# Retention, then a cosine-gated feed-forward: a state tile per head parity, a conversion ahead of two masks, another one part later

## The chip, the cores and the metric

One core of a Trainium2 chip. Times are device microseconds of whole executions. A profiled execution has a span as well (first to last instruction), some 2 us shorter. The chain (the work that ended last, followed back from its end) and the timelines start a group of matmuls at slightly different times, so starts are compared within one view; they are from the chain unless the text says otherwise. Ratios are the mean time of one kernel's fast runs over that of the kernel before in the same rounds, so not quite the ratio of the medians quoted beside them.

Engines: PE is TensorE's matmuls, PEld its weight loads, DVE is VectorE, ACT ScalarE, POOL GpSimd. In a profile line, [0.48 <-DVE stb L491] says that the engine stood idle for 0.48 us until VectorE's instruction of line L491 on tile stb ended; the waits are inferred from semaphore events.

## The reference

```python
def _attn_ref(q, k, v):                       # (4, 8, 768, 64) each
    gamma = 1.0 - 2.0 ** (-5.0 - np.arange(H))
    for t in range(S):
        state = gamma[None, :, None, None] * state + np.einsum('bhd,bhe->bhde', k[:, :, t], v[:, :, t])
        y[:, :, t] = scale * np.einsum('bhd,bhde->bhe', q[:, :, t], state)
def _moe_ref(x, w_in, w_out):                 # (3072, 512), (512, 2048), (2048, 512)
    h = x @ w_in
    return (h * np.cos(h)) @ w_out
```

The retention is computed in chunks of 128 steps: masked scores within a chunk, and a state (64 x 64 per head) from chunk to chunk. Its output is the feed-forward's x.

## The kernel before

A "pair" is one chunk of two batch entries; twelve pairs in a row. Two heads share the 128 partitions: head parity j uses partitions 64j to 64j + 63. The state sums up in one PSUM tile, `st_ps`, as large as each of the seven general banks (512 fp32 per partition), so that here a PSUM tile and a bank are the same thing. Copies bring it to SBUF as bf16 weights for the next pair; the other parity's partitions stay zero.

```python
banks = Banks([psum.tile([128, 512], FP32, name=f"bank{i}") for i in range(7)], clk)
st_ps = psum.tile([128, 2, HP, D], FP32, name="st_ps")
stb = [sb([128, 2, HP, 128], BF16, f"stb{i}") for i in range(2)]
...
def state_out(p, copy_st):                    # later pairs: both copies on one engine
    for j in range(2):
        copy_st(out=stb[(p + 1) % 2][ts(j, 64), :, :, ts(j, 64)], in_=st_ps[ts(j, 64)])
...
it = stage_a(1, 0)                            # scores of pair 1
stage_m(1, it, (0,))                          # mask on VectorE
stage_s(0, None)                              # state after pair 0
for j, cp in enumerate((nc.scalar.copy, nc.vector.tensor_copy)):
    cp(out=stb[1][ts(j, 64), :, :, ts(j, 64)], in_=st_ps[ts(j, 64)])     # L491
stage_m(1, it, (1,))
stage_m(1, stage_a(1, 1))
half_y(0, 0); half_y(0, 1); half_y(1, 0)      # (three lines in the kernel, with clock lines between)
first_f((0, 1), 0)                            # first feed-forward matmuls, L366
...
pair_f(2, 0); conv_k(4, True)                 # two cosines, then k of pair 4 on ScalarE
pair_f(2, 1); conv_k(5, True)                 # two cosines, then k of pair 5
attend(3)                                     # scores and four masks of pair 3
```

`pair_f` makes two PSUM banks of w_in products (L353), each with a cosine on ScalarE (L331) and a product on VectorE (L335) that frees the bank. The cut joins some lines and leaves out the lines that feed the time model (`clk`). The tile framework places all waits. The line numbers in the profiles are the kernel's own.

## Time and profile before

| | kernel before |
|---|---|
| median of 6 runs in the rounds of the result | 208.16 us (207.82 to 208.64) |
| span of the profiled run | 205.8 us |
| TensorE busy, and its share of the chain | 97%, 92% |
| VectorE, ScalarE busy | 55%, 56% |
| first state copies (L491) | ScalarE 12.58 to 13.17 us, VectorE 13.19 to 13.88 us |
| first feed-forward matmuls (L366) | 15.21 us |

From 15.21 us to its last matmul, at 202.7 us, TensorE waits for no other engine on the chain. Only an earlier start, or a new gap, can move that point; the last copy out (202.73) and its store follow. Two weight loads in the timeline of weight loads (columns: start, duration, engine, line, operation) say how finely the framework tracks the state tile:

```profile
13.34 0.11 PEld L283 LDWEIGHTS <-stb 128*64 128x64 bf16 x1
13.94 0.11 PEld L283 LDWEIGHTS <-stb 128*64 128x64 bf16 x1 [0.48 <-DVE stb L491]
```

The first load takes parity 0's columns while VectorE is still writing parity 1's into the same tile; only the second load waits for VectorE.

### The profile page before, as it was taken

How to read it: one execution, taken by the hardware profiler on the slowest of the kernel's cores; microseconds unless marked ns; L12 is line 12 of the kernel's file. 1: busy time of each engine (PE TensorE's matmuls, PEld its weight loads, DVE VectorE, ACT ScalarE, POOL GpSimd, SP SyncE). 2: the span in 40 equal slices, each digit the busy share in tenths (PEclk: the TensorE clock that was granted, in tenths of full speed). 3: DMA queues.
4: the chain of work that ended last, by engine and by line, in shares of the span. 5: the costliest groups of instructions: out<-in, count | busy, mean ns of one | idle time of the engine just before them, and what ended most of it. 6: DMA issues, size and time to landing. Idle time of an engine off the chain costs nothing.

```text
span 205.8 us, 4101 instructions
## 1 busy us (share of the span) xinstructions
PE 199.2 (97%) x1631; PEld 113.0 (55%) x1631; DVE 113.3 (55%) x188; ACT 114.3 (56%) x191; POOL 92.4 (45%) x99
## 2 busy tenths in 40 slices
PE   7889999999999999999999999999999999999993
PEld 2458554558897555556454466444465444444453
DVE  4885884532968545769784366844467233344000
ACT  7675882259887536787446466453554654553120
POOL 8999338399999479979930730000000000000000
PEclk9999999999999999999999999999999999999999
DMA  6999999979999997999999905101101101110212
GB/s 155 352 243 198 217 244 286 341 139 294 319 187 255 338 127 132 312 298 229 251 371 362 194 29 127 53 6 49 51 3 53 51 15 39 51 51 5 99 51 102
DMA packets 33571, 34.34 MB, mean 167 GB/s; under 512 B 23376, under 2 KB 25680, under 8 KB 33552
## 3 DMA queue, kind: packets, MB, share of 16 engines
q0 software_dynamic: 7824, 22.29, 39.2%
q1 hardware_dynamic: 24544, 11.44, 23.6%
q10 hardware_dynamic: 1184, 0.36, 0.7%
q8 instruction: 12, 0.20, 0.4%
q14 instruction: 7, 0.06, 0.1%
HBM read 27.26 MB, written 6.29 MB: 163 GB/s over the span
## 4 chain that ended last, share of the span: by engine, by line
PE 92%; POOL 3%; DMA 2%; DVE 1%; issue 0%; ACT 0%; POOLq 0%
PE bank L388 39%; PE bank L342 32%; PE bank L353 7%; PE bank L261 3%; PE bank L283 3%; PE bank L288 3%; DMA vf<-in_v_dram 2%; PE bank L366 2%; PE bank L408 2%; PE st_ps L305 1%; POOL qf L130 1%; POOL kf L137 1%; POOL vs L204 1%; PE bank L232 0%; POOL kf L130 0%; POOL vf L130 0%
## 5 line engine op out<-in xcount | busy, mean ns | idle before, releaser
L335 DVE TENSOR_TENSOR gt<-bank,cosb 128x512 bf16<-128x512 f32 x96 | 65.1, 689 | 59.4 <-ACT cosb L331 59.2
L331 ACT ACTIVATE cosb<-bank,halfpi 128x512 bf16<-128x512 f32 x96 | 65.0, 687 | 50.0 <-PE bank L342 44.5
L388 PE MATMUL bank<-w_out_sb,gt 128*128 128x512 bf16 x368 | 89.8, 379 | 0.0
L342 PE MATMUL bank<-xt,w_in 128*128 128x512 bf16 x304 | 75.3, 380 | 0.0
L388 PEld LDWEIGHTS <-gt 128*128 128x128 bf16 x368 | 35.4, 98 | 41.1
L342 PEld LDWEIGHTS <-w_in 128*128 128x128 bf16 x304 | 33.9, 114 | 30.5
L270 DVE TENSOR_TENSOR am<-bank,mask 128x512 bf16<-128x512 f32 x48 | 30.5, 682 | 4.0 <-PE bank L261 4.0
L204 POOL TENSOR_TENSOR vs<-vf,gk 128x512 bf16<-128x512 f32 x21 | 21.4, 1046 | 11.3 <-DMA vf<-in_v_dram 9.5
L197 POOL TENSOR_TENSOR qk<-qf,gq 128x512 bf16<-128x512 f32 x18 | 18.8, 1064 | 8.1 <-DMA out_dram<-ob 3.3
L395 ACT COPY ob<-bank 128x512 f32<-128x512 f32 x23 | 13.4, 587 | 14.8 <-PE bank L388 14.4
L210 ACT CAST qk<-kf 128x512 bf16<-128x512 f32 x24 | 13.9, 616 | 11.1 <-DMA kf<-in_k_dram 11.1
L292 ACT CAST xt<-bank 128x512 bf16<-128x512 f32 x24 | 13.0, 591 | 8.3 <-PE bank L288 8.3
L353 PE MATMUL bank<-xt,w_in 128*128 128x256 bf16 x128 | 14.6, 273 | 0.0
L353 PEld LDWEIGHTS <-w_in 128*128 128x128 bf16 x128 | 13.9, 113 | 0.8 <-issue 0.2
L288 PE MATMUL bank<-am,vs 128*64 128x128 bf16 x192 | 11.7, 220 | 0.4 <-DVE am L270 0.4
L317 DVE CAST stb<-st_ps 64x512 bf16<-64x512 f32 x14 | 9.6, 685 | 3.9 <-PE st_ps L305 3.7
L283 PEld LDWEIGHTS <-stb 128*64 128x64 bf16 x160 | 8.8, 109 | 4.7 <-issue 3.8
L283 PE MATMUL bank<-qkt,stb 128*64 128x128 bf16 x160 | 10.8, 222 | 0.3 <-DVE stb L491 0.3
L137 POOL DMA_DIRECT2D kf<-in_k_dram x9 | 10.5, 1172 | 0.0
L288 PEld LDWEIGHTS <-vs 128*64 128x64 bf16 x192 | 9.9, 110 | 0.5 <-issue 0.4
L130 POOL DMA_DIRECT2D vf<-in_v_dram x8 | 7.1, 885 | 4.9 <-DMA w_out_sb<-in_moe_w_out_dram 4.9
L137 POOL DMA_DIRECT2D qf<-in_q_dram x8 | 9.2, 1151 | 0.0
(49 smaller groups left out, 98.7 us busy)
## 6 DMA issues: line engine op xcount, KB each, us to landing
out_dram<-ob SPq DMA_DIRECT2D x23, 256.0 KB, 2.4
kf<-in_k_dram POOLq DMA_DIRECT2D x9, 512.0 KB, 6.3
qf<-in_q_dram POOLq DMA_DIRECT2D x8, 512.0 KB, 7.0
vf<-in_v_dram POOLq DMA_DIRECT2D x8, 512.0 KB, 8.1
vf<-in_v_dram POOLq DMA_DIRECT2D x8, 256.0 KB, 5.4
w_out_sb<-in_moe_w_out_dram POOLq DMA_DIRECT2D x4, 512.0 KB, 12.3
qf<-in_q_dram POOLq DMA_DIRECT2D x6, 256.0 KB, 7.2
w_in<-in_moe_w_in_dram POOLq DMA_DIRECT2D x3, 512.0 KB, 6.3
```

Of the source, the lines that this page charges most:

```text
L137: nc.gpsimd.dma_start(out=both[n][SLOT[p]].rearrange("p b h d -> p (b h) d"), in_=SRC[n][1][2 * bp : 2 * bp + 2, :, ds(c * C, C)].rearrang ...
L197: eng.tensor_tensor(out=qk[p % NB][:, b, 0], in0=qf[SLOT[p]][b], in1=bc(gq, p % NC), op=ALU.mult)
L204: eng.tensor_tensor(out=vs[p % NB][:, b], in0=vf[SLOT[p]][b], in1=bc(gk, p % NC), op=ALU.mult)
L210: nc.scalar.copy(out=qk[p % NB][:, b, 1], in_=kf[SLOT[p]][b])
L270: nc.vector.tensor_tensor(out=am[p % 2][b][j], in0=ap[j], in1=mask.unsqueeze(1).to_broadcast([128, HP, 128]), op=ALU.mult)
L283: nc.tensor.matmul(yp[ts(j, 64), a, :], lhsT=stb[p % 2][:, b, a, ts(j, 64)], rhs=qt(n, b, a), start=True, stop=False, skip_group_check=True)
L288: nc.tensor.matmul(yp[ts(j, 64), a, :], lhsT=vs[n][:, b, 2 * a + j, :], rhs=am[p % 2][b][j][:, a, :], start=(c == 0), stop=True, skip_grou ...
L331: nc.scalar.activation(out=cb, in_=bank, func=AF.Sin, bias=halfpi)
L335: nc.vector.tensor_tensor(out=out, in0=bank, in1=cb, op=ALU.mult)
L342: nc.tensor.matmul(bank, lhsT=w_in_t(i, f), rhs=xt[g % 2][:, i, :], start=(i == 0), stop=(i == KIN - 1))
L353: nc.tensor.matmul(bank[:, ts(e, 256)], lhsT=w_in_t(i, f + e), rhs=xt[g % 2][:, i, ts(hf, 256)], start=(i == 0 and e == 0), stop=(i == KIN ...
L388: nc.tensor.matmul(bank, lhsT=gt[g % 2][:, f, ts(j, 128)], rhs=w_out_sb[:, f, :], start=(f == 0), stop=(f == KOUT - 1))
```

## The change

Its intent: ScalarE and VectorE copy the first state side by side (part 1); the second v conversion of pair 2 fills VectorE's wait for scores (part 2); k of pair 5, whose transfer ScalarE stands waiting for, goes behind the next two cosines (part 3).

```diff
-    stb = [sb([128, 2, HP, 128], BF16, f"stb{i}") for i in range(2)]
+    stb = [[sb([128, 2, HP, 64], BF16, f"stb{i}_{j}") for j in range(2)] for i in range(2)]
...
-                        yp[ts(j, 64), a, :], lhsT=stb[p % 2][:, b, a, ts(j, 64)],
+                        yp[ts(j, 64), a, :], lhsT=stb[p % 2][j][:, b, a, :],
...
-        cp(out=stb[1][ts(j, 64), :, :, ts(j, 64)], in_=st_ps[ts(j, 64)])
+        cp(out=stb[1][j][ts(j, 64)], in_=st_ps[ts(j, 64)])
...
-            conv_v(2, nc.vector, (0,))
+            conv_v(2, nc.vector)
         elif u == 9:
             stage_m(2, stage_a(2, 0))
-            conv_v(2, nc.vector, (1,))
...
     pair_f(2, 1)
-    conv_k(5, True)
     attend(3)
     cq(4)
     stage_t_dma(4)
+    pair_f(2, 2)
+    conv_k(5, True)
...
-    pair_f(2, 2)
     pair_f(2, 3)
```

(The cuts leave out the memsets and the copies of later pairs, which change alike.)

More of the change, by code (lines that the diff above doesn't have):

```diff
@@ L178 @@
         nc.vector.memset(lgv[:, h : h + 1], lg[h])
-    for t in stb:
+    for t in stb[0] + stb[1]:
         nc.vector.memset(t, 0.0)
@@ L316, in state_out @@
         for j in range(2):
-            copy_st(out=stb[(p + 1) % 2][ts(j, 64), :, :, ts(j, 64)], in_=st_ps[ts(j, 64)])
+            copy_st(out=stb[(p + 1) % 2][j][ts(j, 64)], in_=st_ps[ts(j, 64)])
             clk.run("act" if copy_st == nc.scalar.copy else "dve", 0.65, clk.pe + 0.1)
```

## The prediction

> **What bounds the kernel now.** I read the page's busy shares first, then the chain that ended last (totals, then its opening in order of time), then VectorE, ScalarE and weight loads in that opening. The page's first lines:
>
> ```profile
> span 205.8 us, 4101 instructions
> PE 199.2 (97%) x1631; PEld 113.0 (55%) x1631; DVE 113.3 (55%) x188; ACT 114.3 (56%) x191; POOL 92.4 (45%) x99
> ...
> PE 92%; POOL 3%; DMA 2%; DVE 1%; issue 0%; ACT 0%; POOLq 0%
> ```
>
> TensorE is busy 97% of the span and carries 92% of the chain; VectorE holds 1% of it and ScalarE under half a per cent. So shortening work of VectorE, ScalarE or GpSimd pays only where such work is on the chain, and 1% is about 2 us. Where? The chain cut to its opening (columns: start in us, duration in us, engine, tile and line):
>
> ```profile
> 6.21 4.86 DMA vf<-in_v_dram
> 11.06 0.07 issue
> 11.13 1.05 POOL vs L204
> 12.19 0.04 issue
> 12.23 0.33 PE st_ps L305 x8
> 12.55 0.02 issue
> 12.58 0.59 ACT stb L491
> 13.17 0.02 issue
> 13.19 0.69 DVE stb L491
> 13.88 0.03 issue
> 13.91 0.70 DVE am L270
> 14.62 0.04 issue
> 14.66 0.22 PE bank L288
> ...
> 15.21 1.00 PE bank L366 x8
> ```
>
> The reader is to see two state copies (L491) **one after the other**: ScalarE 12.58 to 13.17, VectorE from 13.19. They read different partition halves of one PSUM tile, st_ps, and write different parts of one SBUF tile. Only after VectorE's copy comes the mask (13.91) for which TensorE waits (14.66). From 15.21 on the chain is TensorE alone: it never again leaves it for another engine, up to the end. In its dense stretches (chain, 30.13: 6.91 us for 32 matmuls of 512 columns) a matmul takes 6.91 / 32 = 0.216 us. Nothing in the change removes a matmul, so the only prize is an earlier start of the dense part.
>
> The other places that the change touches lie at 36.9 to 57.1 us, and there TensorE is busy 10.20 of 10.20 us and 10.00 of 10.00 us in the busy times by stretch. The waits that the change aims at are others':
>
> ```profile
> 38.72 0.68 DVE L204 TENSOR_TENSOR vs<-vf,gk 128x512 bf16<-128x512 f32 x1
> 40.02 1.29 DVE L270 TENSOR_TENSOR am<-bank,mask 128x512 bf16<-128x512 f32 x2 [0.61 <-PE bank L261]
> 41.22 0.68 DVE L204 TENSOR_TENSOR vs<-vf,gk 128x512 bf16<-128x512 f32 x1
> 42.18 1.29 DVE L270 TENSOR_TENSOR am<-bank,mask 128x512 bf16<-128x512 f32 x2 [0.28 <-PE bank L261]
> 52.55 1.14 ACT L210 CAST qk<-kf 128x512 bf16<-128x512 f32 x2 [0.70 <-DMA kf<-in_k_dram]
> ```
>
> VectorE waits 0.61 us for scores before it masks, and ScalarE stands 0.70 us in front of a k that has not landed, with its cosines queued behind. Neither delays TensorE today.
>
> **What the Trainium skill says.** (1) "PSUM — Partial Sum Buffer", section "PSUM bank collisions raise a hardware error": two engines on one bank and one group of 32 partitions collide, two reads included; different groups of one bank may be used together; the page calls guarding by whole bank "the simple version". The copies use partitions 0 to 63 and 64 to 127, so the chip would allow them together, but software that guards by bank puts one behind the other, whatever they write. The trace agrees with some such order: a 0.02 us step from one copy to the next. (2) "SBUF — State Buffer", section "Summary: rules for kernel authors": when VectorE has two SBUF inputs and GpSimd reads SBUF, the later one is blocked. The trace fits: GpSimd's q conversion took 1.44 us at 41.37 beside VectorE's v conversion (41.22 to 41.90), against 1.04 us at 39.85, which ran beside masks. (3) "TensorE: Matmul & The Clock Gate", section "Wait — 56ns, not 53.3ns?": 215.7 ns start to start for 512 columns when warm; the trace has 0.216 us, so the dense part has no slack inside.
>
> **Part 1, a state tile per head.** It leaves 18 further copies alike (14 on VectorE at 690 ns median, 4 on ScalarE at 582): from L317, both halves of a pair go to one engine, so no two engines meet. It makes four memsets of half the size from two: 128x512 words took 485 ns, 128x256 words 0.27 us, so 4 x 0.27 - 2 x 0.485 = 0.11 us more on VectorE before 2.4 us, where it then idles 1.67 us for q; ScalarE's tables behind it end at 4.54 and its next work comes at 4.77. Cost: nothing. The prize is L491 alone. If VectorE's copy starts with ScalarE's, at 12.58 or so rather than 13.19, the mask ends 0.61 us earlier. Before it, VectorE's last mask ends at 11.86 + 0.68 = 12.54, so VectorE is free. TensorE is at 13.40 with this product's first half, so 14.66 - 0.61 = 14.05 can be met. The next matmuls (15.21 becomes 14.60) need ScalarE's xt copies, which end at 13.38 + 1.07 = 14.45: 0.15 us of room. w_in's blocks land at 14.4, 15.8 and 18.4 (issue time plus time to landing) and would be needed at 14.6, 16.4 and 19.2. So the whole 0.61 us would reach the dense part.
>
> But does the split remove the wait? A tile-wide order on the destination is the intent's theory. The trace speaks against it: the first state weights (columns of head 0) were loaded at 13.34, **while** VectorE was still writing the same tile (13.19 to 13.88); only the second half's load waited, to 13.94. And vs of pair 0 was written by ScalarE (10.59) and GpSimd (10.45 to 11.06) at once. So dependencies within an SBUF tile look finer than the tile already, and disjoint parts don't wait. What the two copies still share, and the change leaves shared, is the source bank. I choose 6 chances in 10 that the order stays.
>
> **Part 2, v conversion ahead of the masks.** Same four VectorE instructions. The second conversion moves from 41.22 into the idle 0.61 us before the first mask: 38.72 + 2 x 0.68 = 40.08 instead of 40.02 for that mask, 0.06 us later; its product is needed at about 44, so TensorE sees nothing. v's second half has landed by 38.2 (29.06 + 9.1). GpSimd's second q conversion loses its collision: 1.44 - 1.04 = 0.40 us earlier, hence the k fetches behind it by up to that. Direct worth: 0.
>
> **Part 3, k of pair 5 one F part later.** The same two conversions (0.62 us each) go behind the first two cosines of the next part. The cosines no longer sit behind a 0.70 us DMA wait; but VectorE multiplies them only after its masks (to 54.98), and TensorE runs 51.12 to 54.83 for 32 matmuls without a stop. The transposes of pair 5 also need q, converted until 54.12 + 2.05 = 56.17, later than k's new end: the part starts at 51.12, its first two results are there at 52.0 and 52.9 (8 matmuls in 0.87 us each), the second cosine ends at 52.9 + 0.69 = 53.6, and two conversions at 53.6 + 1.14 = 54.7. So k is not late. Direct worth: 0 to 0.1 us.
>
> **Sum.** If the order at L491 goes: 0.61 us less at 14.6, carried on. Parts 2 and 3 then matter as passers-on: TensorE would be at pair 3's products at 54.2 instead of 54.8, and masks and xt copies must follow. k4 lands at 42.75 + 6.8 = 49.55 and gates ScalarE there, so without the 0.40 us from part 2 some of the gain would be lost again; I allow 0 to 0.2 us of loss. That gives 208.18 - 0.6 = 207.6. If the order stays: 208.18 - 0 to 0.1, say 208.15. Weighted: 0.4 x 207.6 + 0.6 x 208.15 = 207.93, rounded to **208.0** as the loss on the way speaks for the upper side.
>
> **The rivals.**
> - *The copies do go side by side* (4 in 10): for it, the step of 0.02 us after ScalarE shows no other cause, and a conservative comparison of two interleaved writes can't be excluded; against it, the weight load at 13.34. Time 207.6.
> - *The wait goes and another takes its place*: xt copies with 0.15 us of room at 14.45, or pair 3's masks and k4's landing at 49.55. Time 207.7 to 208.1.
> - *An engine becomes the bound*: VectorE and ScalarE are at 55 and 56% and lose nothing; k5 late could delay pair 5, whose scores come at 70.35. With 15 us between its conversion and those, unlikely. It would make 208.3 to 208.8.
> - *The two readers of one bank slow each other*: no sign to judge by; at most the 0.69 us grows and eats part of 0.61.
>
> **Range and chances.** The three runs before spread 207.82 to 208.45, so 0.3 us either way is noise, on both branches: 207.6 - 0.3 = 207.3 and 208.15 + 0.35 = 208.5. Two per cent is 4.2 us, seven times the largest prize, so "within 2%" is nearly sure: faster 0.01, same 0.98, slower 0.01.
>
> **What would show it.** In the changed trace: L491 on VectorE starts about 13.2 with a wait on ScalarE (order stays) or about 12.6 (gone). The first matmuls of line L366 start at 15.2 or at 14.6. VectorE shows two v conversions in a row near 38.7 and no wait of 0.7 us for k before the cosines near 52. If L366 starts at 14.6 and the span still is 205.8, the gain was given back between 37 and 57 us, and a TensorE gap must be there. The prediction is wrong if the order is gone and all else holds (nearer 207.5), or if bank choices, which a built-in time model makes anew for part 3, bring a TensorE stall that today is absent.

## The result, and the profile after

Median 208.02 us (207.54 to 208.44, 6 runs) against 208.16 us; ratio 0.9988, 95% interval 0.9968 to 1.0009. No difference can be told. The head of the changed kernel's page, and its chain by engine:

```profile
span 205.9 us, 4080 instructions
PE 197.2 (96%) x1609; PEld 112.5 (55%) x1631; DVE 113.4 (55%) x190; ACT 114.2 (55%) x191; POOL 92.0 (45%) x99
...
PE 91%; DMA 3%; ACT 2%; POOL 2%; issue 1%; DVE 1%; POOLq 0%; ACTq 0%
```

TensorE shows 1609 matmuls for 1631 weight loads: 22 records are missing, and the pieces of "issue" in this chain between matmuls are their places, not waits (0.16 us at 45.28 and then 1.67 us for 7 matmuls of L388, where the kernel before has 1.83 us for 8). VectorE has 2 instructions more, the memsets. The opening of the chain in order of time:

```profile
12.62 0.59 ACT stb L491
13.20 0.02 issue
13.23 0.69 DVE stb L491
...
13.95 0.70 DVE am L270
...
15.25 1.00 PE bank L366 x8
```

The two copies still stand one behind the other, now into two tiles, and VectorE's timeline names what it waited for:

```profile
13.23 0.69 DVE L491 CAST stb<-st_ps 64x512 bf16<-64x512 f32 x1 [0.62 <-ACT stb L491]
```

L366 starts 0.04 us later than before. The lines that parts 2 and 3 were aimed at, from the timelines of VectorE, GpSimd and ScalarE:

```profile
38.76 1.28 DVE L204 TENSOR_TENSOR vs<-vf,gk 128x512 bf16<-128x512 f32 x2
40.06 1.29 DVE L270 TENSOR_TENSOR am<-bank,mask 128x512 bf16<-128x512 f32 x2
...
41.44 1.04 POOL L197 TENSOR_TENSOR qk<-qf,gq 128x512 bf16<-128x512 f32 x1 [0.48 <-DVE am L270]
...
53.85 1.13 ACT L210 CAST qk<-kf 128x512 bf16<-128x512 f32 x2
```

Both v conversions run in a row, the masks follow at once, GpSimd's conversion is back from 1.44 to 1.04 us, and the k conversion no longer waits. All of it happened, and TensorE took none of it up. The k fetch of pair 4 behind GpSimd's conversion went out at 42.42 instead of 42.75 us, but took 7.2 instead of 6.8 us to land: at 49.6 us, no earlier than before.

### The profile page after: what moved, and what is told of

Same layout as the page of the kernel before. It is cut to its first block, busy times and chain, and to the rows that moved or that the text cites. A ratio compares the mean times of both kernels' runs of the same rounds, so it can differ in the third digit from the quotient of the medians.

```text
span 205.9 us, 4080 instructions
## 1 busy us (share of the span) xinstructions
PE 197.2 (96%) x1609; PEld 112.5 (55%) x1631; DVE 113.4 (55%) x190; ACT 114.2 (55%) x191; POOL 92.0 (45%) x99
## 4 chain that ended last, share of the span: by engine, by line
PE 91%; DMA 3%; ACT 2%; POOL 2%; issue 1%; DVE 1%; POOLq 0%; ACTq 0%
PE bank L388 39%; PE bank L342 32%; PE bank L353 7%; PE bank L261 3%; PE bank L283 3%; DMA kf<-in_k_dram 3%; PE bank L288 3%; PE bank L366 2%; PE bank L408 2%; PE st_ps L305 1%; POOL qf L130 1%; ACT vs L222 1%; ACT qkt L235 0%; PE bank L232 0%; POOL kf L130 0%
## 5 line engine op out<-in xcount | busy, mean ns | idle before, releaser
L388 PE MATMUL bank<-w_out_sb,gt 128*128 128x512 bf16 x357 | 88.2, 379 | 0.9 <-issue 0.5
L342 PE MATMUL bank<-xt,w_in 128*128 128x512 bf16 x294 | 74.1, 380 | 0.7 <-issue 0.3
L388 PEld LDWEIGHTS <-gt 128*128 128x128 bf16 x368 | 35.4, 98 | 41.0
L342 PEld LDWEIGHTS <-w_in 128*128 128x128 bf16 x304 | 33.7, 114 | 30.7
L204 POOL TENSOR_TENSOR vs<-vf,gk 128x512 bf16<-128x512 f32 x21 | 21.4, 1045 | 10.4 <-PE bank L342 4.9
L353 PE MATMUL bank<-xt,w_in 128*128 128x256 bf16 x128 | 14.6, 273 | 0.0
L353 PEld LDWEIGHTS <-w_in 128*128 128x128 bf16 x128 | 13.9, 113 | 0.9 <-issue 0.4
```

The lines of the kernel that those rows point to most:

```text
L204: eng.tensor_tensor(out=vs[p % NB][:, b], in0=vf[SLOT[p]][b], in1=bc(gk, p % NC), op=ALU.mult)
L342: nc.tensor.matmul(bank, lhsT=w_in_t(i, f), rhs=xt[g % 2][:, i, :], start=(i == 0), stop=(i == KIN - 1))
L353: nc.tensor.matmul(bank[:, ts(e, 256)], lhsT=w_in_t(i, f + e), rhs=xt[g % 2][:, i, ts(hf, 256)], start=(i == 0 and e == 0), stop=(i == KIN ...
L388: nc.tensor.matmul(bank, lhsT=gt[g % 2][:, f, ts(j, 128)], rhs=w_out_sb[:, f, :], start=(f == 0), stop=(f == KOUT - 1))
```

## The experiments

**Theory:** the shared PSUM bank of the *source* orders the copies. **Rival:** something else does, such as the shared destination or a fixed order of the two engines.

### Two PSUM tiles for the state, with and without the split destination (e1, e2), and the control (e3)

```diff
-    banks = Banks([... for i in range(7)], clk)
-    st_ps = psum.tile([128, 2, HP, D], FP32, name="st_ps")
+    banks = Banks([... for i in range(6)], clk)
+    st_ps = [psum.tile([128, 2, HP, D], FP32, name=f"st_ps{j}") for j in range(2)]
```

and `st_ps[j]` wherever parity j is written or read. So that the kernel keeps to eight PSUM banks in all, the general banks go from seven to six. e1 is this on the changed kernel, e2 on the kernel before with its one interleaved `stb` tile, e3 the changed kernel with six banks only.

> The changed kernel with one PSUM tile (bank) of state per head parity, and six instead of seven general banks. Theory (the shared PSUM bank orders the two copies): VectorE's first state copy starts within 0.1 us of ScalarE's (about 12.6 us instead of 13.2), the first L366 matmul at about 14.6 instead of 15.25 us; total 0.3 to 0.6 us less, or given back by the missing seventh bank. Rival (something else holds VectorE, such as the destination or a fixed order of the engines): VectorE still starts 0.6 us after ScalarE, L366 at 15.2.

> The kernel before, with its single interleaved destination tile kept, and the same two PSUM tiles. Theory: the copies are side by side here too, so a state tile per head is not needed for it: VectorE's copy starts at about 12.6 us, L366 at 14.6. Rival (the shared destination tile orders them as well): VectorE's copy stays 0.6 us behind ScalarE's here, though not in e1.

> The changed kernel with six general PSUM banks and nothing else: what the missing bank costs e1 and e2. Theory: the dense part is bound by TensorE with banks to spare; the first copies and L366 stay at 13.2 and 15.2 us, the total within 0.5 us of the changed kernel. Rival: the bank is needed and TensorE gets gaps, 1 us or more lost.

The two copies in the timelines of VectorE and ScalarE, e1 first, then e2:

```profile
12.50 0.69 DVE L491 CAST stb<-st_ps 64x512 bf16<-64x512 f32 x1
12.47 0.58 ACT L491 CAST stb<-st_ps 64x512 bf16<-64x512 f32 x1
```

```profile
12.45 0.69 DVE L491 CAST stb<-st_ps 64x512 bf16<-64x512 f32 x1
12.42 0.58 ACT L491 CAST stb<-st_ps 64x512 bf16<-64x512 f32 x1
```

Side by side, 0.03 us apart, with either destination. In e3, with six banks and one PSUM tile of state, VectorE again started 0.61 us after ScalarE and waited for it:

```profile
13.18 0.69 DVE L491 CAST stb<-st_ps 64x512 bf16<-64x512 f32 x1 [0.64 <-ACT stb L491]
```

So two source tiles, each in a bank of its own, are enough to lift the order, and a state tile per head parity is not needed for it. Whether the framework goes by the tile or by the bank, these runs don't separate, as each of them is a tile of one bank. L366 started at 14.48 and 14.43 us in e1 and e2, 15.13 in e3 and 15.18 in the changed kernel (timelines of TensorE). Both copies kept their durations beside each other. In e1 and e2 TensorE then waited 0.4 us for GpSimd's v conversion of pair 1 (L204) instead of the mask.

The totals did not follow. e1: ratio 1.0001 (0.9954 to 1.0048), e2: 0.9988 (0.9938 to 1.0039). e3 shows one reason, a line of its waits of TensorE (total us, times, longest):

```profile
PE bank L353 <- DVE gt L335: 0.9, 1, 0.9
```

With six banks TensorE waits for one near 51 us. e3's expectation, banks to spare and a total within 0.5 us, fell in the trace, and the rival came true there: its last matmul group started at 200.38 us instead of the changed kernel's 199.33, 1.05 us later. Timed, e3 was 1.0021 (0.9978 to 1.0065). e1 and e2 carry the same 0.9 us. e2 shows a second reason, in its chain:

```profile
11.98 8.30 DMA w_in<-in_moe_w_in_dram
```

The w_in block for L342, issued at 11.98 us, landed only 8.3 us later, and TensorE waited 1.3 us for it. In the kernel before the same fetch took 6.3 us. At 20.3 us it undid the earlier start. In e1's profile a third part came after TensorE's end: its last store took 2.7 us to land, 1.6 in the kernel before, so that 4.2 us passed from the last copy out (203.43) to the end of the span, against 3.1 (205.8 - 202.73). Its TensorE work ended 0.6 us later than the changed kernel's (last copies 203.43 and 202.86).

### Both first copies on one engine (e6)

```diff
-    for j, cp in enumerate((nc.scalar.copy, nc.vector.tensor_copy)):
+    for j, cp in enumerate((nc.vector.tensor_copy, nc.vector.tensor_copy)):
```

> The changed kernel with both first state copies on VectorE. Theory (the order makes ScalarE's help worthless: 0.58 + 0.69 us one after the other either way): VectorE copies from 12.6 to about 13.95 us, the same end as 13.92 in the changed kernel within 0.1 us, L366 within 0.1 us of 15.25. Rival (two engines do gain something): the end moves to 14.2 us or later.

VectorE copied from 12.33 to 13.74 us and L366 started at 15.07 in the chain: 0.18 us ahead of the changed kernel, where within 0.1 was expected. In the changed kernel ScalarE's copy first waits for its own qkt copy, which ends at 12.60; VectorE was free at the same time there (its masks end at 12.60), but in e6 already at 12.31, since its masks began at 11.03 instead of 11.32 us. So the start of this profile was 0.29 us ahead and the copies gave 0.11 of it back: 1.41 us on one engine (12.33 to 13.74), 1.30 us on two (12.62 to 13.92). While the order stands the second engine brings that 0.1 us at most, in one look.

### The mask into the forced wait (e4, e10 on the changed kernel; e5, e11 on the kernel before)

```diff
     stage_s(0, None)
+    stage_m(1, it, (1,))
     for j, cp in enumerate((nc.scalar.copy, nc.vector.tensor_copy)):
...
-    stage_m(1, it, (1,))
     stage_m(1, stage_a(1, 1))
```

The order of the copies stays; VectorE makes a mask (0.68 us) where it stood still.

> The changed kernel with the one mask that VectorE makes after its first state copy put ahead of it, into the 0.62 us that VectorE waits for ScalarE. The order of the copies stays. Theory: the mask (0.68 us) runs at 12.6 to 13.25, the copy still at about 13.25, TensorE's wait of 0.5 us for the mask goes; L366 starts at 14.6 to 14.7 instead of 15.25, and 0.5 to 0.6 us come off the total (207.5). Rival (gain given back between 37 and 57 us, to late k, masks or xt copies): L366 early, total within 0.2 us of the changed kernel, and a TensorE gap appears before 57 us.

> The kernel before with only the mask put ahead of VectorE's first state copy; parts 1, 2 and 3 of the change are absent. Theory (parts 2 and 3 only pass an earlier start on): L366 starts at 14.6 to 14.7 us as in e4, and 0 to 0.4 us of the 0.6 us are lost again near 50 to 57 us, where ScalarE's conversion of k of pair 5 still stands 0.7 us for its transfer; total between e4 and the kernel before. Rival (parts 2 and 3 do nothing at all): total and span equal e4's within 0.2 us. The landing of the second w_in block, which made TensorE wait 0.6 us in e4, may blur both.

> The changed kernel unaltered, beside e10 and e11 on one chip, because the kernel before spread from 205.5 to 208.0 us of span in the two calls so far and a few tenths can be compared within a call only. Theory (parts 1 to 3 bring nothing): ratio to the kernel before within 0.3% of 1. Rival (a small gain is there): 0.997 or less, interval below 1.

> e4's kernel once more, beside e9. Theory: 0.2 to 0.6 us faster than e9; L366 at 14.6 to 14.7 us, and what TensorE then waits for the second w_in block depends on when that lands (needed at about 19.2). Rival (e4's 0.5% came from slow runs of the kernel before in that call): within 0.1 us of e9.

> e5's kernel once more; in e5's profile VectorE was late from the start (a q block's copy at 11.57 instead of 10.65 us), so it said little of the mask. Theory (parts 2 and 3 pass the earlier start on): L366 at 14.6 to 14.7, and slower than e10 by 0 to 0.4 us, the loss visible in front of L353 near 51 to 57 us. Rival: the same as e10 within 0.1 us and no such gap.

e10's VectorE timeline and chain (the copies are L492 there):

```profile
11.31 1.87 DVE L270 TENSOR_TENSOR am<-bank,mask 128x512 bf16<-128x512 f32 x3
...
12.62 0.59 ACT stb L492
...
13.23 0.70 DVE stb L492
...
14.67 1.00 PE bank L366 x8
```

The copies are where they were in the changed kernel (12.62, 13.23), and L366 starts 15.25 - 14.67 = 0.58 us earlier: the predicted size of the prize, got by another way. Measured:

| kernel | label | median us | ratio to before | 95% interval |
|---|---|---|---|---|
| changed, again | e9 | 208.16 | 1.0007 | 0.9977 to 1.0037 |
| changed + mask first | e10 | 207.56 | 0.9962 | 0.9938 to 0.9986 |
| before + mask first | e11 | 207.56 | 0.9973 | 0.9946 to 0.9999 |
| changed + mask first | e4 | 207.83 | 0.9951 | 0.9915 to 0.9988 |
| before + mask first | e5 | 207.93 | 0.9992 | 0.9959 to 1.0024 |

e9 to e11 shared one chip and the same 11 runs of the kernel before. Changed or not, the mask brings 0.1 to 0.5%, which is clear of noise in e4 and e10 and barely in e11, and small; e5 alone doesn't show it. In e5's profile L366 started only at 15.46 us, against 14.6 to 14.7 expected: three warm-up matmuls had taken 1.49 us at 9.11, as in e9 (last section), and VectorE's masks began at 12.16. e10's median is 0.60 us below e9's, at the upper end of what was expected; e10 and e11 have the same median, as e11's rival said, though e11 too had a gap at L353. The three parts of the change make no difference to it that these runs resolve: the theory that parts 2 and 3 pass the earlier start on found no support.

Part of the start was given back, as e4's rival said, by late k, but also by a cause that it didn't list. In e4 the w_in block landed 7.7 us after its issue at 12.14, and TensorE waited 0.6 us; in e10 it took 6.1 us and nobody waited. In e10 the give-back lies near 51 us; ScalarE's timeline and the chain:

```profile
49.55 1.14 ACT L210 CAST qk<-kf 128x512 bf16<-128x512 f32 x2 [0.48 <-DMA kf<-in_k_dram]
...
50.60 0.69 ACT cosb L331
...
51.31 0.70 DVE gt L335
...
52.05 2.78 PE bank L353 x24
```

ScalarE waits for k of pair **4**, the cosine stands behind it, VectorE's product behind that, and with it the bank that TensorE wants at L353. e4, e10 and e11 lost 0.2, 0.5 and 0.3 us there. Part 3 had moved pair 5's k only.

### k of pair 4 later as well (e12)

```diff
     pair_f(2, 0)
-    conv_k(4, True)
     pair_f(2, 1)
     attend(3)
+    conv_k(4, True)
     cq(4)
```

on top of e10's kernel.

> e4's kernel with ScalarE's conversion of k of pair 4 moved behind the two cosines of the part that it stood ahead of (part 3 had moved the k of pair 5 only). In e4, e10 and e11 TensorE waited 0.2, 0.5 and 0.3 us in front of L353 near 51 to 52 us for a bank that VectorE frees after a cosine that stood behind this k. Theory (the landing of that k takes back part of the earlier start): no wait of L353 for VectorE's gt there, 0.2 to 0.5 us less than e10's kernel: ratio to the kernel before 0.994 to 0.997. Rival (the bank comes late for another reason, VectorE's masks): the wait stays, ratio as e4 and e10 (0.995 to 0.996) or worse. Whether w_in's second block lands after 19.2 us blurs both by up to 0.6 us.

The same stretch of its chain:

```profile
49.98 0.55 PE bank L261 x16
50.53 3.62 PE bank L353 x32
54.15 0.17 PE bank L283 x2
```

The wait is gone, and this profile's span is 205.2 us, 0.6 less than the kernel before's: the whole earlier start (14.61 instead of 15.21) arrives at the end. But in this profile k of pair 4 landed at 42.21 + 6.7 = 48.9 us, against 42.29 + 7.2 = 49.5 in e10. ScalarE's first two cosines ended at 49.0, so in the old order it would not have waited for k either. That the new order would also bear a late k follows from the code, where the cosines no longer stand behind it, but this one look doesn't show it. Timed: median 207.69 us of 6 runs, one of them slow; ratio 0.9974 (0.9940 to 1.0008). Three of the five fast runs were at 206.9 to 207.1 us, the other two at 208.3 and 209.0, so the time is not shown to be better than e10's.

### Parts 2 and 3 by themselves (e7, e8)

> The kernel before with part 2 alone (both v conversions of pair 2 ahead of the masks). Theory: GpSimd's second q conversion near 41.4 us takes 1.04 instead of 1.44 us because VectorE no longer runs a two-input operation beside it, the k fetch behind it is issued 0.3 to 0.4 us earlier; TensorE between 37 and 57 us unchanged, span within 0.3 us of 205.8. Rival: the 1.44 us had another cause and stays.

> The kernel before with part 3 alone (k of pair 5 one F part later). Theory: ScalarE's wait of 0.70 us in front of the conversion at 52.5 us is filled by two cosines, the last two cosines before the xt copies start no earlier than before within 0.2 us, because the order of the work behind them is full; TensorE's L353 after the pair-3 products starts at 57.0 to 57.2, span within 0.3 us of 205.8. Rival: 0.3 us or more come off there.

One look each, so their traces count and not their totals. e7: GpSimd's conversion took 1.04 us, as the theory said; in e8, without part 2, it took 1.43. The k fetch behind it was issued at 42.51 instead of 42.75 us, 0.24 us earlier where 0.3 to 0.4 was expected. It landed 7.5 us later, at 50.0, after the 49.55 of the kernel before, and TensorE waited 0.5 us at L353: an earlier issue did not mean an earlier landing. e8: the wait for pair 5's k was filled as expected and the xt copies started at 56.22, no earlier than before (55.89); L353 behind the products started at 57.39, later than the 57.0 to 57.2 expected, since TensorE had waited 0.2 us for a bank behind pair 4's k. Neither part alone shortened anything in these profiles.

The collision that part 2 removes can also come back elsewhere. In e9, the changed kernel again but 0.5 us later at this place, VectorE's two v conversions met GpSimd's first q conversion and took 2.13 us instead of 1.28:

```profile
39.67 1.21 POOL L197 TENSOR_TENSOR qk<-qf,gq 128x512 bf16<-128x512 f32 x1 [2.05 <-DMA qf<-in_q_dram]
39.30 2.13 DVE L204 TENSOR_TENSOR vs<-vf,gk 128x512 bf16<-128x512 f32 x2
```

And in e11, without part 2, GpSimd's second q conversion took 1.04 us anyway, because the earlier start had moved VectorE's v conversion (40.62 to 41.30) out of its way (41.23).

## Why the prediction was right

- **The number.** That 208.02 came out beside 208.0 is luck. 208.0 is a mean of two branches, 207.6 and 208.15; the branch that happened says 208.15, and the 0.14 us between the two kernels here is within the noise (e9, the same kernel, had a ratio of 1.0007). All six runs of the result lie in 207.3 to 208.5: two of e9's six, 209.32 and 209.54, do not, though their median, 208.16, does.
- **What bounds.** "From 15.21 on the chain is TensorE alone" held up to the last matmul; then follow VectorE's copy at 202.73 and a store, which the prediction left out and which cost 1.1 us more in e1. The one profile with an early L366 and no later wait, e12, ended early. The other losses that were followed up are TensorE waits, for w_in (0.6 and 1.3 us) or a bank (0.2 to 0.9).
- **Part 1.** The choice "that the order stays", 6 in 10, was right, and its ground too: the early weight load spoke against the destination as the cause, and what stayed shared was the source. e1 to e3 show it (as a tile or as a bank is open). The branch with 4 chances, side by side copies, did not happen in the changed kernel.
- **The prize.** 0.61 us was worked out for the start; e10 got 0.58, e1 15.25 - 14.55 = 0.70, this from a profile that was 0.15 us ahead at the copies. What would bind next was missed: the prediction gave xt copies 0.15 us of room, but GpSimd's v conversion of pair 1 ended at 12.94 + 1.06 = 14.00, 0.05 us before the 14.05 that it worked out, and e1 and e2 waited for it.
- **Memsets.** 0.11 us more was worked out, the two groups measured 1.09 against 1.03 us: 0.06. It was hidden, as said.
- **Part 2.** First masks at 40.08 by the sum, 40.06 in the trace; GpSimd 0.40 us shorter, as said; direct worth none.
- **Part 3.** Pair 5's k converted at 54.7 by the sum, 53.85 + 1.13 = 54.98 in the trace, and not late.
- **Passing on.** Mis-sized in thought: "without the 0.40 us from part 2 some of the gain would be lost again". That k of pair 4 gates ScalarE was right, but nothing shows that part 2 helps: its earlier issue gave no earlier landing in the changed kernel and e7, and in e10 and e11 the fetch went out at the same time (42.29 and 42.21 us) with and without part 2; e10 lost 0.5 us there, e11 0.3. With that conversion moved (e12) the wait was absent, with the reserve said there.
- **Noise.** "0.3 us either way" was too small a measure of runs: the kernel before alone went from 207.56 to 209.79 us. The upper end of the range adds 0.35 us and not the 0.3 that is named as noise.

What stays open: whether ScalarE and VectorE could read two partition halves of one bank at once at full speed. The framework orders them (the wait ends with ScalarE's copy), and no run here has them unordered in one bank.

## What to carry to other kernels

When two engines won't run side by side, list everything they share, source as well as destination, and look in the trace for an access that already ignores one of the candidates. A forced wait on an engine can be filled with work that stands just behind it: reordering one mask gained what splitting a tile did not. And follow an earlier start to the end; a transfer that was just in time can become the next wait. When a wait is gone in one profile, look whether the transfer behind it happened to be early.

## What the Trainium skill lacked or had wrong

- "PSUM — Partial Sum Buffer", section "PSUM bank collisions raise a hardware error": it speaks of dependencies by bank and group of 32 partitions. In this kernel two *reads* of different partition halves were ordered, at a cost of 0.61 to 0.62 us, until the halves lay in two tiles of a bank each (0.03 us apart in e1 and e2). The page has no word on what guarding by whole bank costs.
- "TensorE: Matmul & The Clock Gate", section "What's actually happening": it lets the moment at which the clock comes up vary by ±500 ns, because its window runs freely. These profiles of one kernel differ by more: in the changed kernel's first profile one warm-up matmul of 512 columns at 5.83 us already took 0.38 us, while in e9 three at 9.23 us still took 1.40 us, against 0.81 us in the first profile. L366 then started at 15.79 instead of 15.25. That the page's window is the reason, no run here shows. The two lines, first profile and e9:

```profile
8.22 0.81 PE L425 MATMUL bank<-gt 128*128 128x512 bf16 x3
```

```profile
9.23 1.40 PE L425 MATMUL bank<-gt 128*128 128x512 bf16 x3
```

  The granted clock that the profile lists was 1.00 from 8 to 10 us in both, so that column doesn't show it.
- No page that was read gives the spread of one fetch's landing from run to run. The w_in block at 12 us took 6.1 to 8.3 us over these profiles, as much as the whole prize and more.
- "SBUF — State Buffer", section "Summary: rules for kernel authors", on VectorE with two SBUF inputs beside GpSimd, was borne out: GpSimd's conversion took 1.44 and 1.43 us with such a neighbour, 1.04 without (0.40 us more, where VectorE's instruction had 41.90 - 41.37 = 0.53 us left), and in e9 VectorE was the later one, with 2.13 instead of 1.28 us for two.
